# Batch 1's keys and queries loaded by SP, and its means summed on VectorE instead of TensorE

## The chip, the cores and the metric

One core of a Trainium2 chip. The time is the device time of the whole program in microseconds (us). "Span" is the length of one profiled execution, some 1.7 us less than its time. A run is called slow when it is over 1.5% above the fastest of the same kernel.

## What is computed

Sparse attention over 4 batches, 8 heads, 768 positions and 64 dimensions feeds a gated layer with `x` of 3072 x 512. Each query sees the keys within 15 positions and one summary of each block of 32: the maximum of the block's keys, the mean of its values. The part that the change concerns is `v_sum`.

```python
k_sum = k.reshape(B, H, nb, 32, D).max(axis=3)
v_sum = v.reshape(B, H, nb, 32, D).mean(axis=3)
scores_l = scale * np.matmul(q, k.transpose(0, 1, 3, 2))      # masked to |i - j| < 16
scores_s = scale * np.einsum('bhsd,bhnd->bhsn', q, k_sum) + np.log(32)
a = softmax(concat(masked scores_l, scores_s))
x = concat(heads, np.matmul(a, concat(v, v_sum)))
out = (sigmoid(x @ w_gate) * (x @ w_val)) @ w_out
```

## The kernel before

The gated layer of one batch runs on TensorE while the attention of the next batch is slipped between its units. The units of batch 0's layer are `m1` (gate and value products for one of 12 slices and one half of the rows) and `m2` (half of an output tile). `spread(base, extra, lo, hi)` puts the attention's units among them from unit `lo` on. A letter names a unit of attention: T transposes keys and queries on TensorE, K (inside T) expands keys on VectorE, S makes scores and exponentials, A multiplies by the values, X and Y carry the result to `xT` (on TensorE, or by a DMA transpose), V makes the block means on TensorE, and L, R and M make them by a load of rows, ten additions and a scaling on VectorE. Batches 2 and 3 use L, R, M. Batch 1 uses V.

```python
for f in (6, 8, 10):                       # last weights: loaded by SP, cast by GpSimd
    raw = big()                            # one of two 8 KB buffers "vm"
    for o, wb, wap in ((0, wg_bf, moe_w_gate), (1024, wv_bf, moe_w_val)):
        st = view(raw, o, [[256, NP], [1, 256]])
        nc.sync.dma_start(out=st, in_=...)
        copy("pool", wb[:, :, 128 * f:128 * f + 256], st)
held = []
for p in range(NP):                        # batch 1's keys and queries, on GpSimd's queue
    st = staging(6)
    held.append([load_qk(tap, 1, p, st[i], queue=nc.gpsimd) for i, tap in ((0, k), (1, q))])
for i in range(6):
    load_wo(i)                             # GpSimd's queue
for p in range(NP):
    srcs[1][p] = [cast_qk(x, "pool") for x in held[p]]
load_v(1, 0, NQ)                           # GpSimd's queue
...
FIRST = "T0 T1 S0a S0b T2 S1a S1b T3 S2a S2b S3a S3b"
LAST = "V W0 W1 A0 W2 A1 X0 W3 A2 X1 A3 X2 X3"
...
def V(self, *_):
    vsp = ps([128, 512], FP32, "vsp")
    for t in range(NQ):                    # twelve matmuls
        nc.tensor.matmul(out=vsp[96:128]..., lhsT=zband[:, 30 - 2 * t:62 - 2 * t],
                         rhs=vx[0:W, t, :, 0:64], start=(t == 0), stop=(t == NQ - 1))
    ...
def L(self, g, h=None):
    st = self.vm[g] = big()[0:4 * NS]      # the same two "vm" buffers
    nc.sync.dma_start(out=st, in_=v[self.b, 4 * g:4 * g + 4].rearrange("h (n w) d -> n h (w d)", w=32))
def R(self, g, h):
    st = self.vm[g]
    for n in ((1024,), (512, 256, 128, 64))[h]:
        nc.vector.tensor_tensor(out=st[:, 0:n], in0=st[:, 0:n], in1=st[:, n:2 * n], op=ALU.add)
def M(self, g, h=None):
    nc.vector.tensor_scalar_mul(out=mb, in0=self.vm[g][:, 0:64], scalar1=1.0 / 32.0)
    nc.sync.dma_start(out=self.vx[96:120, 0, 4 * g:4 * g + 4, 0:64], in_=mb)
...
    extra = (att[1].units(FIRST) + [lambda: loads(2), lambda: means(2)]   # means(2): L0, L1 of batch 2
             + att[1].units(LAST) + att[2].units(FIRST_KEYS))
    spread(m1[1] + ffn.units2(), extra, 4, 23)
```

The softmax here doesn't subtract the row's maximum and nothing guards it: scores larger than these inputs give would overflow.

Of the kernel before, what the change touches and what calls it, by code (L numbers as in the profile page):

```python
# [16 lines left out]
def kernel(  # L17
# [10 lines left out]
    nc = tc.nc  # L28
# [33 lines left out]
    def view(ap, off, dims):  # L62
        return bass.AP(ap.tensor, ap.offset + off, [list(ap.ap[0])] + [list(d) for d in dims])
# [66 lines left out]
    def load_qk(tap, b, p, st, half=None, queue=None):  # L130

        n = S if half is None else HALF
        s0 = 0 if half is None else HALF * half
        T = n // 128
        (queue or nc.sync).dma_start(  # L135
            out=st.rearrange("p h t d -> p h (t d)"),
            in_=tap[b, 2 * p:2 * p + 2, s0:s0 + n, :].rearrange("h (p t) d -> p h (t d)", t=T),
        )
        return st

    def staging(T):

        raw = small().rearrange("p a c d -> p (a c d)").bitcast(FP32)
        return [view(raw, 128 * T * i, [[64 * T, 2], [64, T], [1, 64]]) for i in range(12 // T)]
# [298 lines left out]
    def spread(base, extra, lo, hi):  # L443

        n, m, j = len(base), len(extra), 0
        for i, u in enumerate(base):
            u()
            if i >= lo:
                want = min(m, (m * (i + 1 - lo) + (hi - lo) - 1) // (hi - lo))
                while j < want:  # L450
                    extra[j]()
                    j += 1
        while j < m:
            extra[j]()
            j += 1
# [4 lines left out]
    att = [Attention(b, srcs[b], xTs[b]) for b in range(B)]  # L460
# [45 lines left out]
    for f in (6, 8, 10):  # L506
        raw = big()
        for o, wb, wap in ((0, wg_bf, moe_w_gate), (1024, wv_bf, moe_w_val)):
            st = view(raw, o, [[256, NP], [1, 256]])
            nc.sync.dma_start(out=st, in_=wap.rearrange("(c p) f -> p c f", p=128)[:, :, 128 * f:128 * f + 256])  # L510
            copy("pool", wb[:, :, 128 * f:128 * f + 256], st)
    held = []
    for p in range(NP):
        st = staging(6)
        held.append([load_qk(tap, 1, p, st[i], queue=nc.gpsimd) for i, tap in ((0, k), (1, q))])
    for i in range(6):
        load_wo(i)
    for p in range(NP):
# [1 line left out]
    load_v(1, 0, NQ)  # L520

    REST = "Q0 Q1 S0b Q2 S1b Q3 S2b S3b A0b A1b X0b A2b X1b A3b X2b X3b"
    FIRST = "T0 T1 S0a S0b T2 S1a S1b T3 S2a S2b S3a S3b"
    LAST = "V W0 W1 A0 W2 A1 X0 W3 A2 X1 A3 X2 X3"

    LATER = """
        0 R0a   1 R0b   2 M0   3 R1a   4 R1b   5 M1   6 K0   8 K1 D2   9 S0a
# [4 lines left out]
    def means(b):  # L532
        if b < B:
            att[b].L(0)
            att[b].L(1)

    def loads(b):
        if b < B:
            srcs[b][0], srcs[b][1] = load_nat(k, b), load_nat(q, b)
            load_v(b, 0, NQ)  # L540

    for b in range(B):
        ffn = f0 if b == 0 else Ffn(b, xTs[b])
        m1 = [[(lambda f=f, hf=hf: ffn.m1(f, hf)) for f in range(NF)] for hf in range(2)]
        if b == 0:
            spread(m1[0][1:], a0.units(REST), 3, 11)
            extra = (att[1].units(FIRST) + [lambda: loads(2), lambda: means(2)]
                     + att[1].units(LAST) + att[2].units(FIRST_KEYS))
            spread(m1[1] + ffn.units2(), extra, 4, 23)
        else:  # L550
            base = m1[0] + m1[1] + ffn.units2()
            at = {i: [] for i in range(len(base))}
            if b + 1 < B:
                for w in LATER.split():
                    if w.isdigit():
                        slot = int(w)
                    else:
                        at[slot] += att[b + 1].units(w)
                at[1].append(lambda: loads(b + 2))
                at[22].append(lambda: means(b + 2))  # L560
            if b + 2 < B:
                at[32] += att[b + 2].units(FIRST_KEYS)
            for i, u in enumerate(base):
                u()
                for x in at[i]:
                    x()
# [30 lines left out]
```

## Time and profile before

| | |
|---|---|
| median of 3 runs | 256.33 us (254.06 to 256.58) |
| profiled run, its span | 254.44 us, 252.7 us |
| TensorE busy | 233.6 us of the span |
| batch 1's first transposes T0 | 56.15 us, after 2.81 us of waiting |
| batch 1's layer begins | 96.25 us |
| from there to the end | 156.45 us |

A line of a timeline reads: start, duration, engine, line of the kernel, operation, output and inputs, shapes, count, and in brackets the idle time before it with what ended it. The prediction below shows the lines.

### The profile page before, as it was taken

Reading aid. Unit: us, or ns where it says so; the run is one execution under the profiler, and the core shown is the slowest. Engines: PE = TensorE matmul, PEld = TensorE weight load, DVE = VectorE, ACT = ScalarE, POOL = GpSimd, SP = SyncE. Lnnn points to the kernel's source line nnn. Section 1 sums busy time; section 2 is a strip of 40 time slices with the busy share of each in tenths; the row PEclk is TensorE's granted clock in tenths of the full one; section 3 lists DMA queues with packets and bytes.
Section 4 is the critical chain, followed back from the end, with each engine's and each line's share of the span. In section 5 each row is a group of like instructions: output and inputs, shape, how many; then the busy total and the mean of one; then the engine's idle time right before and its main releaser. Section 6 shows DMA issues by size and latency. Waiting matters only on the chain.

```text
span 252.7 us, 5164 instructions
## 1 busy us (share of the span) xinstructions
PE 233.6 (92%) x2056; PEld 133.0 (53%) x2056; DVE 133.2 (53%) x269; ACT 109.1 (43%) x196; POOL 94.1 (37%) x131
## 2 busy tenths in 40 slices
PE   1699998958999999998999999999999999999993
PEld 1475565525653555654554456555544466665442
DVE  5875348427882635985853309987643034444000
ACT  2865475516881253355551123555611243333121
POOL 8870369489999998584401000000000000000000
PEclk9999999997999999999999999999999999999998
DMA  6999998999999999999999974160024310000122
GB/s 217 238 166 201 317 307 222 267 341 185 123 124 155 158 191 146 151 177 136 174 175 135 225 182 108 43 129 1 3 74 146 116 41 0 3 0 0 62 107 84
DMA packets 97164, 35.57 MB, mean 141 GB/s; under 512 B 82388, under 2 KB 93172, under 8 KB 96756
## 3 DMA queue, kind: packets, MB, share of 16 engines
q0 software_dynamic: 66336, 14.03, 64.1%
q1 hardware_dynamic: 29716, 20.43, 33.6%
q10 hardware_dynamic: 1088, 0.79, 1.0%
q8 instruction: 16, 0.26, 0.4%
q14 instruction: 8, 0.07, 0.1%
HBM read 34.34 MB, written 6.29 MB: 161 GB/s over the span
## 4 chain that ended last, share of the span: by engine, by line
PE 76%; DMA 11%; ACT 3%; POOL 3%; DVE 3%; issue 2%; SPq 1%; ACTq 0%; POOLq 0%
PE m L430 24%; PE gp L399 21%; PE vp L399 20%; DMA nat<-in_q_dram 7%; DMA vm<-in_moe_w_val_dram 5%; PE sc L257 3%; PE av L342 2%; PE vsp L280 2%; POOL wo L179 1%; ACT kTn L203 1%; PE tp L197 1%; PE m L419 1%; DVE kTx L237 1%; POOL wv L122 1%; SPq L135 1%
## 5 line engine op out<-in xcount | busy, mean ns | idle before, releaser
L407 DVE SCALAR_TENSOR_TENSOR hT<-gate,vp 128x384 bf16<-128x384 f32 x96 | 52.6, 549 | 57.2 <-PE vp L399 54.1
L399 PE MATMUL gp<-xT,wg 128*128 128x384 bf16 x384 | 79.6, 328 | 0.4 <-ACT xT L373 0.2
L399 PE MATMUL vp<-xT,wv 128*128 128x384 bf16 x384 | 78.6, 326 | 0.8 <-DVE hT L407 0.8
L406 ACT ACTIVATE gate<-gp 128x384 f32<-128x384 f32 x96 | 47.3, 492 | 52.8 <-DVE hT L407 33.2
L430 PE MATMUL m<-wo,hT 128*128 128x512 bf16 x276 | 62.7, 380 | 0.0
L399 PEld LDWEIGHTS <-wv 128*128 128x128 bf16 x384 | 37.5, 98 | 26.4 <-issue 1.8
L399 PEld LDWEIGHTS <-wg 128*128 128x128 bf16 x384 | 35.5, 98 | 22.6 <-issue 0.6
L166 POOL DMA_DIRECT2D vx<-in_v_dram x48 | 37.0, 800 | 18.5 <-DMA vx<-in_v_dram 12.1
L430 PEld LDWEIGHTS <-hT 128*128 128x128 bf16 x276 | 25.7, 98 | 29.4 <-issue 0.4
L435 ACT ACTIVATE ot<-m 128x512 f32<-128x512 f32 x23 | 13.7, 597 | 52.8 <-PE m L430 51.2
L263 ACT ACTIVATE P<-sc 128x768 bf16<-128x768 f32 x32 | 25.6, 815 | 11.1 <-PE sc L257 11.1
L264 DVE TENSOR_TENSOR P<-P,mask 128x768 bf16<-128x768 bf16 x32 | 18.7, 590 | 7.1 <-ACT P L263 6.7
L233 DVE TENSOR_REDUCE kTx<-kTn 128x24 bf16<-128x768 bf16 x16 | 15.2, 948 | 9.7 <-ACT kTn L203 6.7
L197 PE MATMUL tp<-ident,qkbf 128*128 128x128 bf16 x96 | 10.3, 271 | 9.7 <-DVE qkbf L120 5.7
L351 DVE TENSOR_TENSOR xs<-av,rec 128x768 bf16<-128x768 f32 (+1 forms) x20 | 16.0, 798 | 0.7
L156 POOL DMA_DIRECT2D nat<-in_q_dram x16 | 13.6, 894 | 2.8 <-DMA nat<-in_k_dram 2.8
L257 PE MATMUL sc<-qT,kTx 64*128 64x64 bf16 x384 | 11.8, 196 | 2.8 <-DVE kTx L237 2.4
L197 PEld LDWEIGHTS <-qkbf 128*128 128x128 bf16 x96 | 8.0, 121 | 11.6 <-DVE qkbf L120 6.2
L257 PEld LDWEIGHTS <-kTx 64*128 64x128 bf16 x384 | 7.9, 97 | 11.8 <-issue 6.3
L156 POOL DMA_DIRECT2D nat<-in_k_dram x16 | 13.4, 890 | 1.1 <-DMA vx<-in_v_dram 1.1
L349 DVE RECIPROCAL rec<-av 128x12 f32<-128x12 f32 (+1 forms) x20 | 4.3, 215 | 15.8 <-PE av L342 15.7
L122 POOL CAST qkbf<-nat 128x768 bf16<-128x768 f32 (+1 forms) x12 | 8.2, 717 | 11.0 <-DMA nat<-in_q_dram 10.9
(58 smaller groups left out, 132.7 us busy)
## 6 DMA issues: line engine op xcount, KB each, us to landing
out_dram<-ot SPq DMA_DIRECT2D x23, 256.0 KB, 3.2
vx<-in_v_dram POOLq DMA_DIRECT2D x40, 96.0 KB, 5.6
vm<-in_v_dram SPq DMA_DIRECT2D x4, 768.0 KB
vm<-in_k_dram SPq DMA_DIRECT2D x4, 384.0 KB, 3.9
vm<-in_moe_w_gate_dram SPq DMA_DIRECT2D x3, 512.0 KB, 4.4
vm<-in_moe_w_val_dram SPq DMA_DIRECT2D x3, 512.0 KB, 5.3
nat<-in_k_dram POOLq DMA_DIRECT2D x4, 384.0 KB, 9.8
nat<-in_q_dram POOLq DMA_DIRECT2D x4, 384.0 KB, 10.1
```

The source lines that it names most:

```text
L156: nc.gpsimd.dma_start(out=nat[:, h // 2, :, 64 * (h % 2):64 * (h % 2) + 64], in_=tap[b, h].rearrange("(c p) d -> p c d", p=128))
L166: nc.gpsimd.dma_start(out=vx_t[b % 2][r0:r0 + hi - lo, t, :, 0:64], in_=v[b, :, lo:hi, :].transpose([1, 0, 2]))
L197: nc.tensor.transpose(dst[:, 128 * t:128 * (t + 1)], src[:, t].rearrange("p h d -> p (h d)"), ident)
L233: nc.vector.tensor_reduce(out=kTx[:, 0, W:KX], in_=kTn[:, 16:16 + S].rearrange("p (n w) -> p n w", w=32), axis=AX.X, op=ALU.max)
L257: nc.tensor.matmul(out=sc[:, i, QT * t6:QT * (t6 + 1)], lhsT=kTx[64 * i:64 * i + 64, t, :], rhs=qT[64 * i:64 * i + 64, QT * t:QT * (t + 1) ...
L263: nc.scalar.activation(out=Ph, in_=sc[:, :, 0:6 * QT], func=ACT.Exp, scale=SCALE)
L264: nc.vector.tensor_tensor(out=Ph, in0=Ph, in1=mask[:, None, 6 * hf:6 * hf + 6, :].rearrange("p i t w -> p i (t w)") .to_broadcast([128, 2, ...
L351: nc.vector.tensor_tensor(out=xs[:, 0:3 * G].rearrange("p (g a) i d -> p g (a i) d", g=G), in0=avf[:, :, :, 0:64], in1=rec[:, 0:G].to_broa ...
L399: nc.tensor.matmul(out=o, lhsT=wb[:, c, 128 * f:128 * (f + 1)], rhs=self.xT[:, c, HALF * hf:HALF * (hf + 1)], start=(c == 0), stop=(c == N ...
L406: nc.scalar.activation(out=gate, in_=gp, func=ACT.Tanh, scale=0.5)
L407: nc.vector.scalar_tensor_tensor(out=self.hT[hf][:, f, :], in0=gate, scalar=1.0, in1=vp, op0=ALU.add, op1=ALU.mult)
L430: nc.tensor.matmul(out=self.m3, lhsT=self.hT[hf][:, f, 128 * tt:128 * (tt + 1)], rhs=wo_bf[:, f], start=(f == 0), stop=(f == NF - 1))
```

## The change

It means to take a wait and one piece of work from TensorE. The loads of batch 1's keys and queries no longer stand in GpSimd's order behind its casts of the weights. V leaves TensorE, and VectorE, half idle, does the sums. The attention starts two units later, and the sums go in among T and S.

```diff
-        held.append([load_qk(tap, 1, p, st[i], queue=nc.gpsimd) for i, tap in ((0, k), (1, q))])
+        held.append([load_qk(tap, 1, p, st[i]) for i, tap in ((0, k), (1, q))])
+    att[1].L(0)
+    att[1].L(1)
     for i in range(6):
         load_wo(i)
@@
-    FIRST = "T0 T1 S0a S0b T2 S1a S1b T3 S2a S2b S3a S3b"
-    LAST = "V W0 W1 A0 W2 A1 X0 W3 A2 X1 A3 X2 X3"
+    FIRST = "T0 T1 S0a S0b R0a T2 R0b M0 S1a S1b R1a T3 R1b M1 S2a S2b S3a S3b"
+    LAST = "W0 W1 A0 W2 A1 X0 W3 A2 X1 A3 X2 X3"
@@
-            spread(m1[1] + ffn.units2(), extra, 4, 23)
+            spread(m1[1] + ffn.units2(), extra, 6, 23)
```

## The prediction

> **What bounds the kernel now.** I read the busy shares and slices first, then the chain of waits, then the timelines of TensorE, GpSimd and VectorE around the weak slices.
>
> ```profile
> PE 233.6 (92%) x2056; PEld 133.0 (53%) x2056; DVE 133.2 (53%) x269; ACT 109.1 (43%) x196; POOL 94.1 (37%) x131
> ...
> PE   1699998958999999998999999999999999999993
> ...
> PEclk9999999997999999999999999999999999999998
> ```
>
> TensorE is the bound: 92% busy, 76% of the chain. Only work taken from TensorE, or a gap in it, can move the end. The slices are 6.3 us; apart from the two ends the weak ones are slice 6 (8), 8 (5) and 9 (8), and slice 9 is the only inner one whose clock fell. The same place in the windows view (us; busy of PE, PEld, DVE, ACT, POOL; granted clock; DMA share; GB/s):
>
> ```profile
> 50.50:53.30 2.80, 2.80 (x18) 1.48 (x16) 1.11 (x2) 1.09 (x3) 2.07 (x3) 1.00 1.03 409
> 53.30:59.05 5.75, 2.75 (x25) 2.06 (x25) 1.01 (x2) 1.28 (x2) 5.24 (x8) 0.77 1.18 258
> 59.05:62.30 3.25, 2.14 (x16) 1.01 (x16) 3.25 (x4) 2.11 (x4) 3.25 (x6) 0.87 1.12 185
> 62.30:74.10 11.80, 11.74 (x166) 7.44 (x166) 10.39 (x23) 10.46 (x17) 11.80 (x16) 1.00 1.86 125
> 74.10:96.25 22.15, 22.15 (x211) 11.01 (x205) 9.07 (x14) 7.24 (x11) 22.15 (x29) 1.00 1.94 163
> ```
>
> TensorE works 2.75 of 5.75 us, then 2.14 of 3.25, at clocks of 0.77 and 0.87. Before 53.3 and after 62.3 it is full. Its timeline says what it waits for:
>
> ```profile
> 56.15 0.57 PE L197 MATMUL tp<-ident,qkbf 128*128 128x128 bf16 x6 [2.81 <-POOL qkbf L122]
> 56.91 2.35 PE L197 MATMUL tp<-ident,qkbf 128*128 128x128 bf16 x18 [0.19 <-POOL qkbf L122]
> 59.05 1.22 PE L399 MATMUL gp<-xT,wg 128*128 128x384 bf16 x4
> ```
>
> These are the transposes of batch 1's first keys and queries, waiting for GpSimd's casts. GpSimd's timeline:
>
> ```profile
> 39.42 1.05 POOL L122 CAST wv<-vm 128x1024 bf16<-128x1024 f32 x1 [0.26 <-DMA vm<-in_moe_w_val_dram]
> 40.42 0.72 POOL L135 DMA_DIRECT2D nat<-in_k_dram  x1
> ...
> 46.08 0.71 POOL L179 DMA_DIRECT2D wo<-in_moe_w_out_dram  x1
> 50.80 0.72 POOL L179 DMA_DIRECT2D wo<-in_moe_w_out_dram  x1 [4.02 <-DMA nat<-in_q_dram]
> ...
> 55.26 6.21 POOL L122 CAST qkbf<-nat 128x768 bf16<-128x768 f32 x8
> ```
>
> Batch 1's eight loads (384 KB each) are issued only after GpSimd has cast the last weights, at 40.4 to 46.1; its next issues, of w_out, wait 4.02 us for those loads to land, and the casts, behind the issues in its order, start at 55.26. TensorE takes each cast tile as it comes.
>
> **What the Trainium skill says.** "TensorE: Matmul & The Clock Gate", Part 1, says an idle window of about 3.4 us halves the clock. The trace agrees in kind: after 2.81 us idle the four matmuls at 59.05 take 1.22 us, against 0.81 elsewhere (both include the last one's latency). "SBUF — State Buffer", SBUF: two separate sides, says VectorE's two-port modes and GpSimd exclude each other for a whole instruction. The trace fits: one kTx copy took 2.32 us while GpSimd cast, and 0.45 to 0.53 later. "DMA: Bandwidth & Descriptors", Queues, rings and completion order, says each engine alternates between queues by packet: SP's loads and GpSimd's issues will share the engines. No row of this trace isolates that. "VectorE: DVE Perf Modes", The perf-mode tier table, gives an fp32 tensor_tensor from SBUF the slowest mode (2,293 ns for 2,048 elements); the trace has 1,215 ns for 1,024.
>
> **The change part by part.**
>
> *The loads move to SP.* SP's last weight issue ends at 34.6 and its staging is free (the half-1 query casts end near 30.5), so the eight loads go out from 34.6, some 0.5 us each (SP's four similar issues took 2.19), to about 39: 6 to 7 us earlier. GpSimd issues the six w_out loads from 40.5 to 44.8 (6 x 0.71) with nothing queued before them, then casts. The last weights (1.05 MB) and the first four of the eight (1.57 MB) at some 300 GB/s, the rate of slices 4 to 8, take 8.7 us from 34.6, so about 43 to 46; the first four casts (0.8 each) are done near 48 to 49.
>
> *First transposes two units later.* The spread now starts after unit 6 instead of 4. The five m1 units at 46.2 to 53.2 become seven, 1.30 each: T0 comes at 53.2 + 2.6 = 55.8, well after its casts. So this gap goes. What it is worth: from 53.3 to the first full run of scores at 62.24 are 8.9 us, in which TensorE did 24 transposes (24 x 0.056 = 1.34, as at 68.04) and one m1 unit (1.30). Hence 8.9 - 2.64 = **6.3 us** lost, by the wait, the slow clock, one cast per 0.77 us and the 2.32 us copy.
>
> *V removed.* Batch 1's means cost TensorE twelve matmuls in series with the rest:
>
> ```profile
> 74.11 2.77 PE L430 MATMUL m<-wo,hT 128*128 128x512 bf16 x12
> 76.81 2.76 PE L280 MATMUL vsp<-vx,zband 96*32 96x512 bf16 x12
> 79.50 2.76 PE L430 MATMUL m<-wo,hT 128*128 128x512 bf16 x12
> ```
>
> From 76.81 to 79.50 that is **2.7 us** of the path. ScalarE's 0.58 us copy goes too, off the path.
>
> *R and M added on VectorE.* Batch 2's sums show their cost:
>
> ```profile
> 98.29 1.22 DVE L314 TENSOR_TENSOR vm<-vm 96x1024 f32<-96x1024 f32 x1
> ...
> 99.89 1.71 DVE L314 TENSOR_TENSOR vm<-vm 96x512 f32<-96x512 f32 x4
> ...
> 101.99 0.19 DVE L318 TENSOR_SCALAR mb<-vm 96x64 bf16<-96x64 f32 x1
> ```
>
> Twice 1.22 + 1.71 + 0.19 is 6.2 us, some 5.8 started back to back. They fall among T, S and m1, where VectorE was busy 10.39 of 11.8 us, so they are not free by themselves. Ledger from T0 at 55.8 to the first A. VectorE, start to start: four K at 1.5 (0.87 + 0.45 + 0.16) = 6.0; five hT at 0.47 = 2.4; eight masks at 0.5 = 4.0; R and M 5.8; together 18.2, from 57.1 (the first keys' copy out of PSUM), so to **75.3**. TensorE: 48 transposes 2.7, five m1 6.5, eight score groups at 0.29 = 2.3, six m2 halves at 1.31 = 7.9; together 19.4, so A at **75.2**. The m2 halves need nothing of VectorE, and moving the spread by two puts three of them among the T and S; that leaves VectorE the time. In order, I expect about 0.5 us before S0 (keys not yet expanded), 0.5 before S3, and at A the wait of the next part: 1 to 2.8 us in all.
>
> *A new path for the means.* M1 ends when VectorE has done all but the last four masks, about 73.3. Its transfer to the vx rows needs 0.8 us to issue (the median there) and, my estimate from the 3.2 us landing of the far larger output transfers, 2.5 to 3 to land: 77. If W0 waits for both halves, A waits 1 to 2 us; if only for its own half, nothing.
>
> *Sum.* 6.3 + 2.7 - (1 to 2.8) = 6.2 to 8.0 us. Batch 1's m1 begins at 88 to 90 instead of 96.25, and the 156 us behind it stay.
>
> **The rivals.**
> 1. *VectorE becomes the bound.* For it: 88% busy in that stretch, and a full order behind each late sum. Against: the ledger balances, 75.3 against 75.2. If each R delayed the hT behind it by its full length, PSUM would hold TensorE back and some 3 us more would be lost: gain about 4, within 2%.
> 2. *The transfers don't come earlier.* The DMA engines are 8 or 9 tenths busy from slice 1 on to past half the span, with the same bytes to move. For it: the means (1.57 MB) sit behind 3.15 MB of keys and queries and would land at about 57 to 63, where the first sum is due at 61 to 62. Being 2 to 4 us late costs about 2 us, as VectorE waits in order. Against harm to T: its four tiles have 7 us of margin.
> 3. *Given back in batch 2.* Its value rows used to be loaded at 36 to 45; now SP can only send them after M1, at about 74, beside the busy small-packet loads (DMA share 1.94). For it: the first sum comes 17 us later, and the keys' transposes already cost VectorE 2.2 us once. Against: outputs of 256 KB land in 3.2 us there, so 1.5 MB should land by 88, and GpSimd's own loads start some 5 us earlier. Loss 0 to 3 us.
> 4. *Only V's share comes off*, the casts being the true limit: 2.7 us, 253.6. Against: T0 comes 7 us after its casts.
>
> **Range and chances.** The middle gain, 7.2 us, is 249.1 from the median of 256.33 and 247.2 from the profiled run of 254.44. I take 248.5, as part of the runs' spread of 2.5 us may come from the wait for landings that goes away. The ledger's edges with a little of rivals 2 and 3 give 246 to 252. Faster by over 2% means below 251.3, a gain of 5.0: 0.83. Within 2%: 0.16, if rivals 1 and 3 come together. Slower: 0.01.
>
> **What will show it.** The waits view should have no qkbf wait of TensorE above 0.5 us and full clock from 50 to 63; T0 near 55.8 with casts done by 50 to 55; no vsp in batch 1; VectorE nearly full from 57 to 75; the gap before the first A under 2 us; batch 1's m1 near 89; from there to the end 156 us. I am wrong if VectorE waits for the value rows, hT falls behind and gp or vp wait for it, or TensorE waits after 96 for batch 2.

## The result

The changed kernel took 248.19 us (median of 4 runs, 246.80 to 249.03), the kernel before in the same rounds 255.88. The ratio of the two is 0.9705, with a 95% interval of 0.9633 to 0.9777: faster by some 7.5 us. A ratio here is the mean time of one kernel's fast runs over that of the other's of the same rounds, so it is not quite the ratio of the medians. In a later set of rounds the same kernel had 248.69 us and 0.9716 (0.9676 to 0.9757).

The page of the changed kernel, the lines of busy time and of slices (each slice 6.2 us):

```profile
PE 228.6 (92%) x2044; PEld 130.7 (53%) x2044; DVE 136.5 (55%) x281; ACT 108.7 (44%) x195; POOL 89.2 (36%) x123
...
PE   1689998999999999999999969999999999999994
...
PEclk9999999999999999999999999999999999999999
```

The 5 of slice 8 and the low clock of slice 9 are gone. A new 6 stands in slice 23, where there was a 9.

The stretches of the changed kernel in the windows view (columns as in the prediction):

```profile
53.30:56.20 2.90, 2.90 (x19) 1.74 (x18) 1.11 (x2) 1.28 (x3) 1.04 (x3) 1.00 1.08 243
56.20:76.86 20.66, 19.82 (x222) 11.53 (x219) 19.08 (x40) 15.03 (x24) 16.54 (x21) 1.00 1.81 151
```

TensorE is full at full clock up to 56.2, where it waited before. From 56.2 to the first A at 76.86, VectorE is busy 19.08 of 20.66 us and TensorE still 19.82. Batch 1's layer begins at 88.32, which is 7.93 us earlier. From profile to profile everything up to here shifts by up to 1.8 us: the second half of batch 0's `m1` begins between 45.05 and 46.82 in the fourteen profiles. Counted from that point, batch 1's layer comes after 41.67 us in place of 50.03, so 8.4 us came off.

GpSimd's timeline says why there was nothing to wait for:

```profile
40.85 4.23 POOL L179 DMA_DIRECT2D wo<-in_moe_w_out_dram  x6
45.04 3.93 POOL L122 CAST qkbf<-nat 128x768 bf16<-128x768 f32 x5
```

The six issues of w_out run through without a wait, and five of the eight casts are done by 49, the last by 56.0. T0 starts at 56.21.

VectorE's timeline, the new sums and what follows:

```profile
69.44 1.22 DVE L314 TENSOR_TENSOR vm<-vm 96x1024 f32<-96x1024 f32 x1
...
72.31 1.70 DVE L314 TENSOR_TENSOR vm<-vm 96x512 f32<-96x512 f32 x4
...
74.15 1.96 DVE L264 TENSOR_TENSOR P<-P,mask 128x768 bf16<-128x768 bf16 x4
76.14 1.26 DVE L120 COPY vx<-vx 24x1408 bf16<-24x1408 bf16 x2
76.86 0.58 PE L342 MATMUL av<-vx,P 120*64 120x65 bf16 x24
```

The last line is TensorE's: A follows the masks and the first copies of the means with no idle time noted. The means' own transfer held nothing up: TensorE's only waits from T0 to batch 1's layer are 0.32 and 0.25 us before the first scores and 0.27 us before the last ones.

But the end came only 5.4 us earlier in this profile (less than the 7.5 us of all runs, as the profiled run of the kernel before, 254.44, was one of its faster ones and that of the changed kernel, 249.03, the slowest of its four). From batch 1's layer to the end it took 158.98 us (247.3 - 88.32) in place of 156.45. One wait of TensorE and GpSimd's timeline show where:

```profile
145.01 0.32 PE L399 MATMUL gp<-xT,wg 128*128 128x384 bf16 x1 [2.41 <-DMA xT<-xs]
```

```profile
91.10 0.74 POOL L166 DMA_DIRECT2D vx<-in_v_dram  x1 [7.90 <-DMA nat<-in_q_dram]
...
129.65 4.10 POOL L156 DMA_DIRECT2D nat<-in_q_dram  x5 [10.72 <-DMA nat<-in_k_dram]
...
157.24 0.72 POOL L166 DMA_DIRECT2D vx<-in_v_dram  x1 [1.62 <-PE gp L399]
```

Batch 2's layer waits for its last input, transposed by a DMA issued at 135.54 that the wait's end puts at 9.5 us. GpSimd pauses twice, for 7.9 and 10.7 us, each time within 9 us of SP's sending two loads of value rows (76.4 and 110.9). Before, there was one such pause (10.66 us, after the loads at 118.2), and GpSimd was done at 137. Now it is not done until 158. This is the part of the gain that was given back, and what the later experiments are about.

### The profile page after: what moved, and what is told of

Same layout as the page of the kernel before. It is cut to its first block, busy times and chain, and to the rows that moved or that the text cites. A ratio compares the mean times of both kernels' runs of the same rounds, so it can differ in the third digit from the quotient of the medians.

```text
span 247.3 us, 5161 instructions
## 1 busy us (share of the span) xinstructions
PE 228.6 (92%) x2044; PEld 130.7 (53%) x2044; DVE 136.5 (55%) x281; ACT 108.7 (44%) x195; POOL 89.2 (36%) x123
## 4 chain that ended last, share of the span: by engine, by line
PE 69%; DMA 13%; DVE 8%; ACT 4%; issue 2%; SPq 1%; POOL 0%; ACTq 0%; DVEq 0%
PE m L430 20%; PE vp L399 20%; PE gp L399 20%; DMA xT<-xs 4%; DMA kTn<-nat 3%; DMA vm<-in_moe_w_val_dram 3%; DMA nat<-in_q_dram 3%; PE av L342 3%; PE sc L257 2%; DVE vm L314 2%; DVE hT L407 2%; DVE kTx L233 1%; ACT kTn L203 1%; PE tp L197 1%; PE vsp L280 1%
## 5 line engine op out<-in xcount | busy, mean ns | idle before, releaser
L264 DVE TENSOR_TENSOR P<-P,mask 128x768 bf16<-128x768 bf16 x32 | 19.3, 614 | 5.8 <-ACT P L263 5.7
L314 DVE TENSOR_TENSOR vm<-vm 96x1024 f32<-96x1024 f32 (+4 forms) x30 | 16.9, 565 | 0.6
L197 PE MATMUL tp<-ident,qkbf 128*128 128x128 bf16 x96 | 8.9, 253 | 6.7 <-DVE qkbf L120 5.9
```

Of the source, the lines that this page charges most:

```text
L264: nc.vector.tensor_tensor(out=Ph, in0=Ph, in1=mask[:, None, 6 * hf:6 * hf + 6, :].rearrange("p i t w -> p i (t w)") .to_broadcast([128, 2, ...
```

## The experiments

Two groups: which part of the change is worth what (e1 to e4, e7), and what the late wait is (e5, e6, e8 to e11). Ratios are to the kernel before, in the same rounds, from fast runs; medians are of all runs. The three right columns are from one profile each.

| run | median us | ratio, 95% interval | T0 to batch 1's layer, us | from there to the end, us | late wait, us |
|---|---|---|---|---|---|
| before (profile) | 255.88 | 1 | 40.10 | 156.45 | none |
| changed, again (e0) | 248.69 | 0.9716, 0.9676 to 0.9757 | 31.81 | 160.49 | 2.37 |
| e1 loads only | 249.38 | 0.9768, 0.9701 to 0.9835 | 37.69 | 156.23 | none |
| e2 loads and spread | 250.08 | 0.9796, 0.9742 to 0.9851 | 35.80 | 157.89 | 1.14 |
| e3 spread only | 250.59 | 0.9820, 0.9755 to 0.9885 | 35.76 | 157.59 | 1.77 |
| e4 means only | 255.50 | 0.9991, 0.9938 to 1.0044 | 38.10 | 158.07 | 2.88 |
| e7 no sums of batch 1 | 248.77 | 0.9718, 0.9675 to 0.9761 | 31.81 | 160.22 | 2.99 |
| e5 no rows of batch 2 | 247.25 | 0.9663, 0.9615 to 0.9712 | 31.89 | 157.34 | 2.44 |
| e6 rows of batch 2 twice | 259.57 | 1.0128, 1.0069 to 1.0186 | 31.80 | 174.46 (slow run) | 2.06 |
| e8 three buffers | 247.29 | 0.9665, 0.9625 to 0.9704 | 32.24 | 158.11 | 1.76 |
| e9 no rows of batch 3 | 245.88 | 0.9636, 0.9598 to 0.9675 | 31.80 | 157.57 | 1.75 |
| e10 outputs earlier | 253.15 | 0.9898, 0.9859 to 0.9936 | 32.58 | 163.61 | 5.79 in three |
| e11 e8 and e10 together | 252.51 | 0.9901, 0.9864 to 0.9938 | 32.30 | 163.49 | 5.12 in two |

The column from T0 may be compared only where the spread begins at the same unit: in before, e1 and e4 T0 stands two `m1` units (2.6 us) earlier in the order. From the start of the second half of batch 0's `m1` to batch 1's layer it is 50.03 us before, 41.67 and 41.36 in the changed kernel (e0 last), 44.65 in e1, 45.35 in e2, 45.31 in e3 and 50.30 in e4.

**The changed kernel again (e0).** No edit.

> The changed kernel again, so that the runs of this call have it in the same rounds: 247 to 249 us. Its first profile had batch 1's first layer at 88.3 us (7.9 earlier) but an end only 5.4 earlier, with one wait of TensorE of 2.4 us for batch 2's transposed inputs at 145 us; I expect that wait in some executions and not in others.

It gave 248.69 us, and the late wait was there again, 2.37 us. With one profile per set of runs, whether some executions go without it is not shown. TensorE's timeline shows a second price of such a wait, which the first profile did not pay:

```profile
142.91 0.32 PE L399 MATMUL gp<-xT,wg 128*128 128x384 bf16 x1 [2.37 <-DMA xT<-xs]
143.07 0.81 PE L399 MATMUL vp<-xT,wv 128*128 128x384 bf16 x4
143.72 1.38 PE L399 MATMUL gp<-xT,wg 128*128 128x384 bf16 x4
144.89 1.48 PE L399 MATMUL vp<-xT,wv 128*128 128x384 bf16 x4
146.17 1.34 PE L399 MATMUL gp<-xT,wg 128*128 128x384 bf16 x4
```

Three groups of four take 1.34 to 1.48 us in place of 0.81; the granted clock from 143.72 to 147.35 is 0.53. From 143.07 the next six groups take 4.93 us, where the first profile, after a wait of 2.41 us, took 3.25 for the same six. So one wait costs 2.4 us in one execution and 4.1 in another.

**One part at a time (e1 to e4).** e1 is the kernel before with the first line of the diff alone (no `queue=nc.gpsimd`). e2 adds the last (`4, 23` to `6, 23`). e3 has the last alone. e4 is the changed kernel with both of these undone, so the means alone.

> One part alone: batch 1's keys and queries on SP, everything else as before (V on TensorE, spread from unit 4). My theory: the gap at 53.3 to 62.2 us comes from the late loads and casts and is worth 6.3 us, so T0 starts at 53.2 to 54 us without a wait above 0.5 us, the clock stays at 1.00, and the time falls by 5 to 6.3 us to about 250. Rival 4 (the casts or transfers are the true limit and the loads are hidden anyway): below 1 us gained and a qkbf wait of about 2.8 us stays.

The time fell by 2.3%, or 5.9 us (0.0232 of the mean before, 255.2). In its profile 5.4 us are gone by batch 1's layer (44.65 us in place of 50.03).

```profile
45.21 5.50 POOL L122 CAST qkbf<-nat 128x768 bf16<-128x768 f32 x7
53.78 1.50 PE L197 MATMUL tp<-ident,qkbf 128*128 128x128 bf16 x24
```

There is no wait for a cast, and seven casts run through from 45.2. The clock in this stretch is 1.00, and over the whole span the runs of e1 to e3, where the wait is gone, have 0.996 to 1.000, those of the kernel before in the same rounds 0.983 to 0.987, and those of e4, where it stays, 0.984 to 0.992. The theory of the gap holds.

> The loads on SP and the spread from unit 6, V kept on TensorE. Theory: once the casts are early, the two units of delay are worth nothing more: within 1 us of e1. Against the full change this run has V's 2.7 us, so the full change should be 1 to 2.7 us faster than this; if the sums on VectorE or batch 2's later value rows take back all of V's share, the two are equal.

As expected, nothing more than e1 (medians 0.7 us apart, intervals overlapping). To the changed kernel there are 0.8 to 0.9% (0.9796 against 0.9705 and 0.9716, other rounds), some 2 us: V's share, less what is given back later. TensorE's timeline has V in series there as before:

```profile
72.46 2.76 PE L280 MATMUL vsp<-vx,zband 96*32 96x512 bf16 x12
```

From T0 to batch 1's layer e2 takes 35.80 us and the changed kernel 32.11 and 31.81, so 3.7 to 4.0 us less, not 2.7. Besides V's 2.7, the scores took 2.5 us of TensorE in place of 3.1, the two groups of a pair now standing together; what else is in the remaining 0.4 to 0.7 was not looked into. Later the changed kernel gives 1.1 to 2.6 us of it back (158.98 and 160.49 against 157.89).

> The spread from unit 6 alone, loads on GpSimd as before, V kept. Theory: two m1 units (2.6 us) fill the wait of 2.8 us, but the casts still run from 55.3 to 61.4 at 0.77 us each and still slow the 2.3 us copy on VectorE, so a gain of about 3 us, half of the 6.3. Rival: if the gap were only a matter of order, this alone gains the same 5 to 6 us as e1; if the wait only moves, below 1.

This missed: 1.8%, some 4.6 us, not 3. Two views suggest why. GpSimd's casts, at 55.26 before, and SP's load of batch 2's value rows, at 36.48 before:

```profile
51.01 6.21 POOL L122 CAST qkbf<-nat 128x768 bf16<-128x768 f32 x8
```

```profile
72.50 0.36 SPq L437 DMA_DIRECT2D out_dram<-ot  x1
73.03 1.74 SPq L306 DMA_DIRECT2D vm<-in_v_dram  x2
```

SP takes its work in the order of the program. Starting the spread two units later puts these loads (2 x 768 KB) behind the first output, which SP cannot issue before it is made, at 72.5. So the edit of one number took 1.57 MB out of the way of batch 1's keys and queries, and the casts came 4.3 us earlier although their loads were issued at 40.1 as before. T0, now two units later, waited for nothing. That the moved rows made the casts earlier is read from this order; no run moves them alone. e2 and e3 have the late wait and e1, with these rows loaded at 41, does not, but e5 below has it without these rows, so they are not its only cause.

> The means on VectorE alone, V gone from TensorE, loads on GpSimd and spread from unit 4 as before. Theory: 2.7 us off TensorE less 0.5 to 1 us of new waits on VectorE, and up to 2.4 us lost later as batch 2's value rows come at about 75 us: a gain of 0 to 2.2 us. Rival 1 (VectorE becomes the bound when the sums are added): slower than before, by 1 to 3 us, with gp or vp waiting for hT between 60 and 75 us.

No gain and no loss (0.9991). The gap is still there, and larger, in TensorE's timeline:

```profile
57.73 3.11 PE L197 MATMUL tp<-ident,qkbf 128*128 128x128 bf16 x24 [5.08 <-POOL qkbf L122]
```

V's 2.7 us was replaced by a longer wait for the casts (5.08 us against 2.81) and a late wait of 2.88. With the spread from 4, seven `m1` units come after T0 and the sums fall among them; VectorE was busy 14.86 us of the 15 from 62 to 77, and TensorE 13.53: here rival 1 is close to true. It is not in the full change (e7), where the sums are mixed with m2 units. That the later start is what makes the difference is not shown: e4's casts are late too, and a run with early loads, the sums and the spread from 4 was not made.

**Are the sums on VectorE free in the full change? (e7)** The additions of batch 1 are left out. Its output is wrong, which doesn't matter for the time.

```diff
             st = self.vm[g]
+            if self.b == 1:
+                return
             for n in ((1024,), (512, 256, 128, 64))[h]:
```

> The changed kernel without batch 1's ten additions on VectorE (5.5 us of it; its means are then single rows, wrong on purpose; loads, scaling and transfers stay). Theory (the ledger): VectorE has room for them, so TensorE's stretch from T0 to batch 1's first layer, 32.1 us in the changed kernel's profile, shortens by less than 1 us, and the time by less than 1 us. Rival 1 (VectorE is the bound there): 3 us or more shorter.

0.9718 against 0.9716, and 31.81 us from T0 to batch 1's layer in both. Leaving out ten additions, which brought VectorE's busy time in this stretch from 25.13 us (e0) to 21.05, changed nothing there, so VectorE has the room that the ledger gave it and rival 1 falls.

**What the late wait is (e5, e9, e6).** In e5 batch 2's value rows are not loaded (its sums run on what the buffers hold), in e9 batch 3's are not; in e6 batch 2's are loaded twice.

```diff
     def means(b):
         if b < B:
+            if b == 2:                          # e9: b == 3, att[3] and att[2]
+                att[2].vm = dict(att[1].vm)
+                return
             att[b].L(0)
             att[b].L(1)
```

> The changed kernel without the two loads of batch 2's value rows (768 KB each, at 76 us): its sums run on what is left in the buffers, so batch 2's result is wrong on purpose. Theory: those loads, moved from 36-46 us into the stretch full of GpSimd's small-packet loads, push batch 2's and 3's keys, queries and values back and cause the 2.4 us wait at 145 us: without them that wait is gone, GpSimd's last issue comes 5 us or more before 157 us, and the time falls by 1 to 2.4 us. Rival: the wait is chance or comes from the earlier start of the batch itself: no change.

The medians differ by 1.4 us (247.25 against 248.69); the intervals overlap. The 7.9 us pause of GpSimd after 83 is gone and it is done at 140 instead of 152 to 158. But the wait itself stayed, 2.44 us. Half of the expectation missed: these loads lengthen GpSimd's work, yet are not by themselves the cause of the wait.

> The changed kernel without the loads of batch 3's value rows (768 KB twice at 111 us; batch 3's sums run on what is left, wrong on purpose). In the changed kernel GpSimd's issues pause 10.7 us after these loads start and are still going at 157 us. Theory: the pause comes from them; without them GpSimd is done by about 140, the output transposes at 136 land in time, the 2.4 us wait at 145 is gone and the time falls by 2 to 2.5 us, to about 246. Rival: the wait comes from the transposes' own queue: it stays, and the time with it.

0.9636, or about 2 us below the changed kernel by the ratios, and GpSimd's timeline has no long pause after 111:

```profile
118.11 5.73 POOL L156 DMA_DIRECT2D nat<-in_q_dram  x7 [1.84 <-DMA nat<-in_k_dram]
...
132.77 0.72 POOL L166 DMA_DIRECT2D vx<-in_v_dram  x1 [0.47 <-issue]
142.24 0.32 PE L399 MATMUL gp<-xT,wg 128*128 128x384 bf16 x1 [1.75 <-DMA xT<-xs]
```

So the pauses do come from SP's row loads: in e5 the first pause is gone and the second is there (11.55 us), in e9 the second is gone and the first is there (7.18). The time of e9 came as expected, but the wait only shrank to 1.75 us (last line, TensorE's). Of all profiles, only before and e1 have no late wait.

What was in flight says more than when GpSimd issued. From the issue of the last transpose to TensorE's use of it, before and e1 took 6.9 us without a wait, and in this stretch GpSimd's queue moved 7 and 1,016 packets. In the nine fast profiles with one late wait it took 8.2 to 10.0 us, and GpSimd's queue moved 3,440 to 4,670 packets meanwhile; in e9, whose last issue ended at 133.5, it was still 4,180. So the transposes are late where GpSimd's loads of many small packets are still landing beside them. In these runs the two go together; a run that takes those loads away and leaves the rest was not made, so the cause is not shown, and the length of the wait is not explained.

> The changed kernel with the loads of batch 2's value rows made twice (1.57 MB more at about 77 us, result unchanged). Theory: the wait for batch 2's transposed inputs, or waits for its keys before it, grow by 3 to 6 us, and the time rises by as much, to 251 to 254. Rival (the later rows are hidden): within 1 us of the changed kernel.

11 us worse than the changed kernel, not 3 to 6. The profile fell in a slow run (clock 0.979), so only its order of events is read:

```profile
74.73 15.14 SPq L306 DMA_DIRECT2D vm<-in_v_dram  x4
...
96.24 1.22 DVE L314 TENSOR_TENSOR vm<-vm 96x1024 f32<-96x1024 f32 x1 [7.47 <-DMA vm<-in_v_dram]
...
97.98 1.44 PE L399 MATMUL vp<-xT,wv 128*128 128x384 bf16 x4 [6.63 <-DVE hT L407]
```

SP needs 15 us for its four issues. VectorE stands 7.5 us before the first sum, hT behind it is late, and TensorE waits 6.6 us; later it waits 4.64 us for batch 2's values (GpSimd's loads). This is rival 3 as the prediction drew it. In the changed kernel there is no such wait: the rows arrive in time. The run is no clean doubling, as the second load of a buffer may have to follow the first, and part of SP's 15 us may be that.

**Two versions meant to hide it (e8, e10).** e8 gives the rows a third buffer (one output buffer less makes the room) so that half of batch 2's rows can be loaded at 40 us, behind batch 1's.

```diff
-    vm_pool = ctx.enter_context(tc.tile_pool(name="vmp", bufs=2))
+    vm_pool = ctx.enter_context(tc.tile_pool(name="vmp", bufs=3))
-    ot_pool = ctx.enter_context(tc.tile_pool(name="otp", bufs=4))
+    ot_pool = ctx.enter_context(tc.tile_pool(name="otp", bufs=3))
@@ L
+            if g in self.vm:
+                return
@@
     att[1].L(1)
+    att[2].L(0)
```

> A version meant to beat both: a third 8 KB staging buffer (and one output buffer less for the room), so that the first half of batch 2's value rows is loaded at about 41 us as before, behind batch 1's, and only the second half at 68. Theory: the wait at 145 us is gone or half, 1 to 2 us faster than the changed kernel, 245.5 to 247.5. Against: the early load makes batch 1's rows or tiles late; then VectorE waits for rows at 62 us and it is no faster.

247.29 us (246.38 to 247.64), correct, 0.9665: 1.4 us below the changed kernel's median in the same rounds, though the intervals overlap at 0.9676 to 0.9704. Its median is the lowest of the correct versions. The wait was 1.76 us; that it is shorter for this reason is not shown, as it was 2.4 to 3.0 us in three profiles of kernels with the same loads of rows (changed, e0, e7).

e10 moves A and Y of the next batch two units ahead (`21 S3b A0 22 Y0 23 A1 ...` in place of `23 A0 24 Y0 25 A1 ...`), and e11 does so on top of e8.

> The changed kernel with the outputs of attention and their transposes (A and Y of the batch ahead) two units earlier, which gives the last transposed input 2.6 us more before the next batch's first layer. Theory: the 2.4 us wait is hidden, whatever causes it: 1.5 to 2.4 us faster than the changed kernel, about 246.3. Against: A on VectorE now falls among the last hT and masks, and those delays take up to 1 us back.

This missed badly: 253.15 us, and three waits for transposed inputs of 0.82, 2.32 and 2.65 us. SP's timeline:

```profile
122.34 1.25 SPq L361 DMA_TRANSPOSE xT<-xs  x1
123.63 2.10 SPq L306 DMA_DIRECT2D vm<-in_v_dram  x2
...
128.65 4.94 SPq L361 DMA_TRANSPOSE xT<-xs  x1
134.32 5.34 SPq L361 DMA_TRANSPOSE xT<-xs  x1
```

The loads of batch 3's rows stand at unit 22 of the order. With the first transpose at 22 too, SP reaches them only after it, at 123.6 in place of 110.9, and they run right into the transposes, whose issues take up to 5.34 us in place of 1.26. The edit moved a second thing, as in e3, and by this order it is the likely cause. e11 did the same:

> The three staging buffers of e8 and the earlier outputs of e10 together, a version meant to beat both kernels. Theory: both act on the same late wait, so the sum is less than the parts: 245 to 246.5 us.

It took 252.51 us (0.9901), with the same order: its rows went out at 123.3, and the issues of its transposes took up to 6.16 us. A version that moves the transposes and leaves the rows where they were was not run.

## Why the prediction was right

- **What bounds it, and the gap.** Right. The loads are issued at 35.9 to 40.9 (34.6 to 39 was forecast), four casts are done by 48 to 49, T0 starts at 56.21 (55.8), and the 6.3 us of the gap measured 5.9 us by e1's runs, 5.4 by its profile. The 6.3 also counted short waits before the first scores that remain without the gap (0.28 and 0.29 us in e1). Rival 4 (only V's share comes off) falls with e1.
- **First transposes two units later.** Unneeded for the gap, as e2 against e1 shows. In the full change it should give room, as it mixes the sums with m2 units, and e4 without it has VectorE full; this is argued, not shown. What I did not see is that it also moves batch 2's row loads behind the first output in SP's order.
- **V.** 2.7 us in series on TensorE, as e2's profile shows. From T0 to batch 1's layer 3.7 to 4.0 us came off, as the scores also take less when their groups stand together.
- **VectorE's ledger.** It said 75.3 against 75.2; VectorE's last mask ended at 76.1 and the first A was at 76.86. e7 shows that the sums cost TensorE nothing there. Rival 1 falls. The waits before S0 and S3 were 0.57 and 0.27 us (0.5 and 0.5 were forecast).
- **The means' path.** The 1 to 2 us at A did not come: the prediction left open whether W0 waits for both halves. The half that W0 and W1 read was sent at 68.02, the other at 74.5, and W0 ran at 76.14 right behind the masks. So all waits together were 0.84 us in place of 1 to 2.8, and the gain up to batch 1's layer was 7.9 us by the clock of the profile, 8.4 and 8.7 (e0) counted from the same unit: at or above the upper edge of 6.2 to 8.0.
- **The rest stays at 156 us.** This step failed. It measured 158.98 and 160.49, by a late wait of 2.4 us and, in one profile, the slow clock after it. Rival 3 had a loss of 0 to 3 us on its list, from row loads at about 75 beside GpSimd's loads, but looked for the harm at batch 2's first sums and keys. It came at batch 2's transposed inputs, stayed without the rows of batch 2 (e5), and was not in the sum. The last sign of being wrong, "TensorE waits after 96 for batch 2", came true.
- **The sum.** 248.5 was forecast and 248.19 measured. The one term too small (no wait at A) and the one left out (the late wait) pull against each other, so that the sum came within 0.3 us is in part luck. (2% of 256.33 is 5.1 us, so "faster" begins at 251.2, not 251.3.)
- **What the page on SBUF says.** "SBUF — State Buffer", SBUF: two separate sides, has VectorE's two-port copies and GpSimd exclude each other. The trace agrees in kind: the first kTx copy took 2.32 and 2.31 us where GpSimd was casting (before, e4) and 0.45 to 0.49 where it was not (the changed kernel, e1, e3). The 1.9 us more are over two casts of 0.77 us, so more than the length of one cast was lost; no run here shows how the turns fall.

Open: what causes the late wait and sets its length, and whether it could be hidden by earlier transposes alone. That the runs before differ by 3.5 us (253.44 to 256.94 in the second set) while the changed kernel's lie within 1.5 in the same rounds fits a wait that goes away, but was only argued.

## What to carry to other kernels

A queue that is issued in order is part of the schedule: two of the edits here that seemed to move one thing also moved a load behind or ahead of something else, by the traces once to the good (e3) and once to the bad (e10), so look at that engine's timeline after every change of order. Here work could be shifted to an engine that was 88% busy in that stretch (92% after it): the ledger of both engines, over the same stretch, still closed, and enough units of the bound engine needed nothing from it. When a gain at one stage is larger than at the end, subtract stage by stage, and look for the wait that was not there before.

## What the Trainium skill lacked or had wrong

- Lacking in "DMA: Bandwidth & Descriptors": what two large loads on SP's queue do to GpSimd's small ones. After 1.57 MB from SP, GpSimd's issues paused for 7.9 and 10.7 us; without the first loads the first pause was gone (e5), without the second the second (e9).
- No page has GpSimd's own issues waiting for its earlier loads to land: 4.02 us ahead of the second load of w_out, and the casts behind it in GpSimd's order late by as much.
- "TensorE: Matmul & The Clock Gate", Part 1, gives an idle window of about 3.4 us before the clock halves, and calls it free-running. Here 2.37 us of idle were followed by three slow groups (1.34 to 1.48 us for 0.81, granted clock 0.53) in one run, and 2.41 us by none in another; in the kernel before, 2.81 us were followed by a clock of 0.87 (59.05 to 62.30). So in these runs a wait below the window's length cost the clock in some cases and not in others.
- No page has the time of DMA transposes beside other loads: 8.2 to 10.0 us from issue to use where GpSimd's queue moved 3,440 packets or more meanwhile, against 6.9 us or less where it moved 7 and 1,016; and beside SP's row loads, issues of 1.2 to 1.3 us became up to 5.34 (e10) and 6.16 (e11).
